# Attention, top-k and a small MLP on one core: another order of the score products, an earlier start of the next keys, and other forms of VectorE's side steps

## The chip, the cores and the metric

The kernel runs on one NeuronCore of a Trainium2 chip. The metric is device time in microseconds (us) of one launch, the median of several runs. The profile is one further execution, taken by the hardware profiler. The engines are called PE (TensorE; PEld is its weight load), DVE (VectorE), ACT (ScalarE), POOL (GpSimd) and SP (SyncE, which here only issues DMAs).

## The reference

Four batches are computed, each with 12288 queries of 128 channels. The keys and values are 4x4 means of a 384x32 grid, multiplied by one 128x128 matrix, so there are 768 of them per batch, and keys equal values.

```python
kv_flat = kv.reshape(B, H // 4, 4, W // 4, 4, C).mean(axis=(2, 4)).reshape(B, -1, C) @ w_sr
s = (q @ kv_flat.transpose(0, 2, 1)) / np.sqrt(C)
a = np.exp(s - s.max(-1, keepdims=True)); a /= a.sum(-1, keepdims=True) + 1e-09
x = a @ kv_flat                                   # (4, 12288, 128)
scores = np.einsum('bsd,d->bs', x, w_gate)        # then, per batch, the 128 highest rows:
xe = x[b, top_idx]; ye = np.maximum(xe @ w1, 0.0) @ w2
out[b, top_idx] = xe + ye / (1.0 + np.exp(-scores[b, top_idx]))[:, None]
```

## The kernel before

The queries are taken in blocks of 256 (two tiles of 128), 48 blocks to a batch, 192 in all. The main loop (from line 732) does one block `i` per turn, and every engine executes its instructions in exactly the order of this program text: the class `InOrder` chains them, and its one call site is line 56, which is why every row of the profile says L56. "Block 2.4" below is block 4 of batch 2, both counted from 0.

In turn `i` the engines do the following. DVE takes the row maximum of block i's scores (`s_max`, tile `m`). PE multiplies attention and values of block i-4 (`AV`, tiles `at` and `vx`, into the two PSUM banks `o_two`), first the high halves (12 products of 259 columns), then the low halves (12 of 130 columns). PE then computes the scores of block i+1 (`S`, into three PSUM banks, `s`), in four parts: part 3 of 512 columns, part 2 of 256, then, after two transposes, part 1 of 256 and part 0 of 512. Each part is the sum of three products, because a score is wanted to nearly fp32 exactness: one fp32r product of the rounded operands (`kh` and `qh`, called HIGH in the change) and two bf16 products of the remainders (`kl` with `qb`, which is the upper half of `qh` read as bf16, and `kb` with `ql`; called LOW). The two transposes (`turn_pe`, rows `s<-cst,am`) turn a 256-column share of block i's exponentials in batches 0 to 2; in batch 3 there are none (`TURN`, line 41) and DMA turns everything. ACT takes the exponentials (`exp`, tile `am`) and their fp16 high halves, POOL subtracts these for the low halves (`hl`, its longest step) and splits queries (`ql`, in even blocks), SP issues the DMA transposes (`turn`), the loads and the stores.

```python
for i, (w, x) in enumerate(high + low if part in (2, 0) else low + high):
    r = pe.matmul(s_flat[n % 2][:, lo:hi], w[:, q], x[:, k], start=(i == 0), stop=(i == 2))
```

Three side jobs are generators. Each stops at named points ("pe", "ev", "up", "g", "t", "cmp", "v", "d"), and `at_point` in the main loop lets the front one of each list go one step on where its point's name comes up, so that a job is spread over many blocks. The "d" point stands at the end of a turn, behind POOL's `hl`.

- `next_keys` (lists `prep` and `vals`) makes the next batch's keys and values: POOL adds up the loaded grid (`kv_sum`), six steps to each of six key tiles, one step a block; PE projects (`key_tile`); at the end `v_split` finds a power-of-two scale per batch and splits the values into fp16 high and low halves (`vx`), with one ACT and two POOL instructions in each of four steps. For batches 2 and 3 the adds wait for six "d" points first (line 350). `AV` of the first block of a batch, four blocks into the batch, needs all of `vx`.
- `topk` (list `select`) is started at the end of block 3 of the following batch. It sets `th` and `tl` on POOL, makes integer keys of the scores on DVE at the "d" point of block 4 (`key`, two instructions), and then searches the threshold, one bit in two or so blocks' points, until about block 37.
- `pick` continues it: it finds the positions of the 128 rows with small products and compares (`ge`, `oh`, `rj`, `idx`), gathers the rows by an indirect DMA of POOL, and runs the MLP. Its last sum is `y * g` on ACT (`xo`), `+ xe` on POOL one step later, and the indirect store of POOL one step after that. For batches 0 and 1 this end falls into blocks 2 to 4 of the batch after the next; for batch 2 it falls into the kernel's tail (`choose` with `drain`).

Batch 3's own selection (`choose`) is the tail, after the last block.

Of the kernel before, what the change touches and what calls it, by code (L numbers as in the profile page):

```python
# [6 lines left out]
F32 = mybir.dt.float32  # L7
# [3 lines left out]
I32 = mybir.dt.int32  # L11
U32 = mybir.dt.uint32
U16 = mybir.dt.uint16
AF = mybir.ActivationFunctionType
ALU = mybir.AluOpType
# [4 lines left out]
P = 128  # L20
# [6 lines left out]
JPC = CHUNK // P  # L27
# [7 lines left out]
NCOL = N // P  # L35
# [7 lines left out]
class InOrder:  # L43


    last = {}
# [24 lines left out]
def attention_topk_mlp(ctx, tc, a, outs, capacity):  # L71
# [108 lines left out]
    def v_split(b):  # L180
# [11 lines left out]
        dve.tensor_scalar(out=mg, in0=mg, scalar1=2.0 ** -96, scalar2=None, op0=ALU.max)  # L192
        dve.tensor_scalar(out=sg[:, 0:2].bitcast(I32), in0=mg.bitcast(I32), scalar1=0x7F800000, scalar2=0x7F800000, op0=ALU.bitwise_and, op1=ALU.bitwise_xor)
        yield "d"
        dve.tensor_scalar(out=sg[:, 0:2], in0=sg[:, 0:2], scalar1=4096.0, scalar2=None, op0=ALU.mult)
# [19 lines left out]
    def first_keys():  # L215
# [85 lines left out]
        S(1)  # L301
# [35 lines left out]
    def next_keys(b):  # L337
# [12 lines left out]
        lead, wait = (2, 0) if b == 1 else (1, 6)  # L350
# [57 lines left out]
    st = {}  # L408
# [15 lines left out]
    def S(n, parts=(0, 1, 2, 3), apart=()):  # L424
        b, blk = blocks[n]
        kh, kl, kb = (kvset[b][x] for x in ("kh", "kl", "kb"))
        qh, qb, ql = qsplit[b, blk]
        assert b == 0 or kvset[b].get("split") == KT
        for part in parts:
            lo, hi, j, k0 = ((0, 512, 0, 0), (512, 768, 0, 512), (768, 1024, 1, 0), (1024, 1536, 1, 256))[part]  # L430
            q = slice(j * P, (j + 1) * P)
            k = slice(k0, k0 + hi - lo)
            low, high = [(qb, kl), (ql, kb)], [(qh, kh)]
            for i, (w, x) in enumerate(high + low if part in (2, 0) else low + high):
                r = pe.matmul(s_flat[n % 2][:, lo:hi], w[:, q], x[:, k], start=(i == 0), stop=(i == 2))
                for y in apart:
                    tc.declare_no_dep(r.ins, y, reason="other banks")

    def s_max(n):
        m = sm.tile([P, QT], F32, name="m")  # L440
        dve.tensor_reduce(out=m, in_=s_flat[n % 2].rearrange("p (j k) -> p j k", j=QT), axis=AX.X, op=ALU.max, negate=True)
        st[n] = {"m": m}
# [145 lines left out]
    def pick(b, mask):  # L588
# [25 lines left out]
        for j0 in range(0, capacity, P):  # L614
# [5 lines left out]
            if j0:  # L620
                yield "d"
                jr = tk.tile([P, P], DT, name="jr")
                dve.tensor_scalar(out=jr, in0=small, scalar1=float(j0), scalar2=None, op0=ALU.add)
            for s in range(2):
                dve.tensor_scalar(out=ge[0:NCOL, s], in0=jr[0:NCOL], scalar1=ecol[0:NCOL, s:s + 1], scalar2=None, op0=ALU.is_ge)
# [20 lines left out]
            dve.scalar_tensor_tensor(out=rj, in0=jcol, scalar=float(j0), in1=row[:, 0:1], op0=ALU.add, op1=ALU.subtract)  # L646
# [5 lines left out]
            dve.scalar_tensor_tensor(out=idx, in0=pj, scalar=float(JPC), in1=row[:, 1:2], op0=ALU.mult, op1=ALU.add)  # L652
# [46 lines left out]
            if last:  # L699
                dve.scalar_tensor_tensor(out=xo[0:n], in0=y_ps[0:n], scalar=g[0:n], in1=xe[0:n], op0=ALU.mult, op1=ALU.add)  # L700
            else:
                act.activation(xo[0:n], y_ps[0:n], AF.Copy, scale=g[0:n])
                yield "d"
                pool.tensor_tensor(out=xo[0:n], in0=xo[0:n], in1=xe[0:n], op=ALU.add)
# [27 lines left out]
    for i in range(nb):  # L732
# [32 lines left out]
        if more:  # L765
            if not old:
                warm(12, s_flat[(i + 1) % 2][:, 1024:1024 + P], bank0 + bank1)
            S(i + 1, (3,), bank0 + bank1)
            S(i + 1, (2,), bank0)
# [4 lines left out]
        if more:  # L774
            S(i + 1, (1,), bank0)
            S(i + 1, (0,))
# [289 lines left out]
```

## Time and profile before

| | us |
|---|---|
| median of 3 runs | 937.86 (934.89 to 938.34) |
| the profiled execution | 938.39 |
| its span, first to last instruction | 936.5 |
| PE busy in the span | 878.3 (94%) |
| DVE busy | 805.6 (86%) |
| POOL busy | 749.0 (80%) |
| ACT busy | 740.7 (79%) |
| mean granted TensorE clock | 0.991 of 2.4 GHz |

A busy PE counts each product until its modelled end, and successive products overlap; how fast PE really goes is read from the distance between starts. Idle time of an engine costs nothing unless another one waits for it.

### The profile page before, as it was taken

The numbers are of one execution on the slowest core, as the hardware profiler recorded it, in microseconds if no ns is written. First come the engines' busy times: TensorE is split into PE (matmuls) and PEld (weight loads), VectorE is DVE, ScalarE is ACT, GpSimd is POOL, SyncE is SP. The second block draws the span as 40 slices with busy tenths as digits, with TensorE's granted clock in tenths as the row PEclk, the third lists the DMA queues.
The fourth block names the chain that finished last, engine by engine and source line by source line (L and its number), as shares of the span: only waits on it lengthen the run. The fifth ranks groups of instructions, "written<-read, shape, count | busy, mean of one in ns | idle before, by whom it ended". The sixth has DMA issues, their size and how long they took to land.

```text
span 936.5 us, 21381 instructions
## 1 busy us (share of the span) xinstructions
PE 878.3 (94%) x7785; PEld 685.6 (73%) x7785; DVE 805.6 (86%) x1929; ACT 740.7 (79%) x1139; POOL 749.0 (80%) x489
## 2 busy tenths in 40 slices
PE   4899999999999999999989999999997999999966
PEld 3577777777777777777767777777785777777766
DVE  5788888898898998999878999999978999999943
ACT  2788888889888887888868888888896999888821
POOL 2699999979788988987886998989887777777732
PEclk9999999999999999999999999999999999999989
DMA  8999999999999999999998999999998999999970
GB/s 318 292 204 232 254 232 243 226 206 202 219 213 224 243 225 230 253 213 253 215 213 181 248 215 230 242 239 241 228 201 189 243 219 250 243 250 259 237 163 27
DMA packets 564125, 211.12 MB, mean 225 GB/s; under 512 B 532368, under 2 KB 533648, under 8 KB 563376
## 3 DMA queue, kind: packets, MB, share of 16 engines
q1 hardware_dynamic: 563696, 209.06, 107.7%
q8 instruction: 62, 1.02, 0.5%
q0 software_dynamic: 320, 0.66, 0.3%
q14 instruction: 47, 0.39, 0.1%
HBM read 52.04 MB, written 25.49 MB: 83 GB/s over the span
## 4 chain that ended last, share of the span: by engine, by line
PE 59%; DVE 20%; DMA 8%; ACT 5%; POOL 4%; issue 2%; DVEq 0%; POOLq 0%; SPq 0%; another core or an unknown queue 0%; ACTq 0%
PE s L56 32%; PE o_two L56 27%; DVE m L56 8%; DMA at<-hl 7%; ACT am L56 3%; POOL hl L56 3%; DVE o_two L56 2%; DVE rz L56 2%; DVE hl L56 1%; DVE x L56 1%; ACT hl L56 1%; DVE key L56 1%; DMA kv_raw<-in_kv 1%; DVE at L56 1%; POOL ql L56 1%
## 5 line engine op out<-in xcount | busy, mean ns | idle before, releaser
L56 POOL TENSOR_TENSOR hl<-am,hl 128x1280 bf16<-128x1280 f32 x192 | 504.3, 2627 | 133.0 <-ACT hl L56 102.4
L56 PE MATMUL o_two<-vx,at 128*128 128x259 f16 (+1 forms) x4548 | 424.1, 247 | 17.0 <-DMA at<-hl 8.6
L56 PEld LDWEIGHTS <-at 128*128 128x128 f16 (+1 forms) x4656 | 365.3, 98 | 101.9 <-DMA at<-hl 18.5
L56 ACT ACTIVATE am<-s,m 128x512 f32<-128x512 f32 (+1 forms) x528 | 358.3, 706 | 62.3 <-DVE m L56 46.3
L56 DVE TENSOR_REDUCE m<-s 128x2 f32<-128x1536 f32 x192 | 336.2, 1751 | 12.5 <-PE s L56 11.5
L56 PE MATMUL s<-kl,qh 128*128 128x512 bf16 (+1 forms) x769 | 253.0, 332 | 0.0
L56 PE MATMUL s<-kh,qh 128*128 128x512 f32 (+1 forms) x769 | 251.5, 408 | 1.4 <-ACT kh L56 0.7
L56 PE MATMUL s<-kb,ql 128*128 128x512 bf16 (+1 forms) x769 | 248.7, 327 | 1.3 <-POOL ql L56 1.3
L56 ACT CAST hl<-am 128x1280 f16<-128x1280 f32 x192 | 241.6, 1258 | 6.1
L56 PEld LDWEIGHTS s<-kh,qh 128*128 128x128 f32 x769 | 131.6, 191 | 31.8 <-ACT kh L56 1.0
L56 DVE TENSOR_REDUCE o_two<-o_two 128x258 f32<-128x516 f32 x188 | 128.3, 683 | 0.0
L56 POOL TENSOR_TENSOR ql<-q_raw,qh 128x512 bf16<-128x512 f32 x96 | 122.7, 1278 | 3.4 <-ACT qh L56 3.4
L56 PEld LDWEIGHTS <-qh 128*128 128x128 bf16 x769 | 74.9, 97 | 62.1 <-issue 61.4
L56 ACT CAST at<-s 128x256 f16<-128x256 f32 x144 | 53.7, 373 | 64.4 <-PE s L56 64.4
L56 DVE TENSOR_SCALAR rz<-o_two,sg 128x2 f32<-128x2 f32 x189 | 41.1, 217 | 47.2 <-PE o_two L56 45.8
L56 PEld LDWEIGHTS <-ql 128*128 128x128 bf16 x769 | 76.2, 99 | 5.2 <-POOL ql L56 2.1
L56 DVE TENSOR_TENSOR x<-o_two,rz 128x256 f32<-128x256 f32 x189 | 78.3, 414 | 0.0
L56 DVE TENSOR_TENSOR at<-s,at 128x256 bf16<-128x256 f32 x144 | 60.7, 422 | 10.4 <-ACT at L56 4.9
L56 PE MATMUL s<-cst,am 128*128 128x128 f32 x288 | 56.2, 277 | 10.0 <-ACT am L56 9.7
L56 ACT CAST qh<-q_raw 128x512 fp32r<-128x512 f32 x96 | 58.8, 613 | 0.0
L56 POOL TENSOR_TENSOR kv_sum<-kv_raw 128x256 f32<-128x256 f32 x72 | 52.6, 730 | 0.0
L56 PEld LDWEIGHTS s<-cst,am 128*128 128x128 f32 x288 | 34.8, 141 | 17.0 <-ACT am L56 15.5
(163 smaller groups left out, 545.8 us busy)
## 6 DMA issues: line engine op xcount, KB each, us to landing
out<-x SPq DMA_DIRECT2D x96, 256.0 KB, 3.1
q_raw<-in_q SPq DMA_DIRECT2D x94, 256.0 KB, 3.7
kv_raw<-in_kv SPq DMA_DIRECT2D x37, 512.0 KB, 4.7
at<-hl SPq DMA_TRANSPOSE x384, 4.0
kv_raw<-in_kv SPq DMA_DIRECT2D x5, 1024.0 KB, 9.5
w<-in_w SPq DMA_DIRECT2D x2, 512.0 KB, 12.1
kv_raw<-in_kv SPq DMA_DIRECT2D x2, 256.0 KB, 5.4
q_raw<-in_q SPq DMA_DIRECT2D x1, 512.0 KB, 5.5
```

What stands on the lines that cost most here:

```text
L56: r = f(*args, **kwargs)
```

## The change

The score products of a turn are put in another order: LOW of parts 3 and 2, HIGH of parts 3 and 2, the two transposes, HIGH of parts 1 and 0, LOW of parts 1 and 0; `S` now makes one part's HIGH or LOW products at a call. `next_keys` of batches 2 and 3 waits for five "d" points instead of six. In `v_split` three DVE instructions on two columns become two each on one column. In `pick`, `ge` also writes a row sum that nobody reads (`took`), `rj` and `idx` become `tensor_scalar` with a per-partition scalar instead of `scalar_tensor_tensor` with a second tensor, and the last sum of the MLP becomes one DVE instruction that reads the product from PSUM, for all batches; with it one "d" step goes.

```diff
--- before.py
+++ after.py
@@ -189,10 +189,14 @@
         mg = kvs.tile([P, 2], F32, name="mg")
         dve.tensor_reduce(out=mg, in_=ps, axis=AX.X, op=ALU.max)
         yield "d"
-        dve.tensor_scalar(out=mg, in0=mg, scalar1=2.0 ** -96, scalar2=None, op0=ALU.max)
-        dve.tensor_scalar(out=sg[:, 0:2].bitcast(I32), in0=mg.bitcast(I32), scalar1=0x7F800000, scalar2=0x7F800000, op0=ALU.bitwise_and, op1=ALU.bitwise_xor)
+        one = [slice(i, i + 1) for i in range(2)]
+        for i in one:
+            dve.tensor_scalar(out=mg[:, i], in0=mg[:, i], scalar1=2.0 ** -96, scalar2=None, op0=ALU.max)
+        for i in one:
+            dve.tensor_scalar(out=sg[:, i].bitcast(I32), in0=mg[:, i].bitcast(I32), scalar1=0x7F800000, scalar2=0x7F800000, op0=ALU.bitwise_and, op1=ALU.bitwise_xor)
         yield "d"
-        dve.tensor_scalar(out=sg[:, 0:2], in0=sg[:, 0:2], scalar1=4096.0, scalar2=None, op0=ALU.mult)
+        for i in one:
+            dve.tensor_scalar(out=sg[:, i], in0=sg[:, i], scalar1=4096.0, scalar2=None, op0=ALU.mult)
         dve.tensor_scalar(out=sg[:, 3:4], in0=sg[:, 0:1], scalar1=float(TAPS), scalar2=None, op0=ALU.mult)
         yield "d"
         parts = [(raw[:, :, 2 * P:2 * P + 1], slice(0, KT), slice(C, VL), 1)]
@@ -298,7 +302,10 @@
         first([(512, 768, 0, 512, True), (1280, 1536, 1, 512, True)])
         project_v(4)
         project_v(5)
-        S(1)
+        for parts in (0, 1), (2, 3):
+            for term in LOW, HIGH:
+                for part in parts:
+                    S(1, part, term)
 
     v_ps = o_two[:, :, 0:3 * (C + 1)].rearrange("p b (t c) -> p b t c", t=3)
 
@@ -347,7 +354,7 @@
                 pend.extend([lambda: None,
                              lambda: (split_k(b, 2 * pair, 2 * pair + 2, 0), split_k(b, 2 * pair, 2 * pair + 2, 1))])
 
-        lead, wait = (2, 0) if b == 1 else (1, 6)
+        lead, wait = (2, 0) if b == 1 else (1, 5)
         raws[0] = load_kv(b, 0, 1 if b == 1 else -2)
         if b == 1:
             raws[1] = load_kv(b, 1)
@@ -421,25 +428,28 @@
 
     blocks = [(b, blk) for b in range(B) for blk in range(NBLK)]
 
-    def S(n, parts=(0, 1, 2, 3), apart=()):
+    LOW, HIGH = 0, 1
+
+    def S(n, part, terms, apart=()):
         b, blk = blocks[n]
         kh, kl, kb = (kvset[b][x] for x in ("kh", "kl", "kb"))
         qh, qb, ql = qsplit[b, blk]
         assert b == 0 or kvset[b].get("split") == KT
-        for part in parts:
-            lo, hi, j, k0 = ((0, 512, 0, 0), (512, 768, 0, 512), (768, 1024, 1, 0), (1024, 1536, 1, 256))[part]
-            q = slice(j * P, (j + 1) * P)
-            k = slice(k0, k0 + hi - lo)
-            low, high = [(qb, kl), (ql, kb)], [(qh, kh)]
-            for i, (w, x) in enumerate(high + low if part in (2, 0) else low + high):
-                r = pe.matmul(s_flat[n % 2][:, lo:hi], w[:, q], x[:, k], start=(i == 0), stop=(i == 2))
-                for y in apart:
-                    tc.declare_no_dep(r.ins, y, reason="other banks")
+        lo, hi, j, k0 = ((0, 512, 0, 0), (512, 768, 0, 512), (768, 1024, 1, 0), (1024, 1536, 1, 256))[part]
+        q = slice(j * P, (j + 1) * P)
+        k = slice(k0, k0 + hi - lo)
+        begun = ("S", part) in st.setdefault(n, {})
+        st[n]["S", part] = True
+        mm = [(qh, kh)] if terms == HIGH else [(qb, kl), (ql, kb)]
+        for i, (w, x) in enumerate(mm):
+            r = pe.matmul(s_flat[n % 2][:, lo:hi], w[:, q], x[:, k], start=not begun and i == 0, stop=begun and i == len(mm) - 1)
+            for y in apart:
+                tc.declare_no_dep(r.ins, y, reason="other banks")
 
     def s_max(n):
         m = sm.tile([P, QT], F32, name="m")
         dve.tensor_reduce(out=m, in_=s_flat[n % 2].rearrange("p (j k) -> p j k", j=QT), axis=AX.X, op=ALU.max, negate=True)
-        st[n] = {"m": m}
+        st.setdefault(n, {})["m"] = m
 
     def by_pe(n):
         return TURN[blocks[n][0]][n % 2] > 0
@@ -621,8 +631,9 @@
                 yield "d"
                 jr = tk.tile([P, P], DT, name="jr")
                 dve.tensor_scalar(out=jr, in0=small, scalar1=float(j0), scalar2=None, op0=ALU.add)
+            took = tk.tile([P, 2], F32, name="took")
             for s in range(2):
-                dve.tensor_scalar(out=ge[0:NCOL, s], in0=jr[0:NCOL], scalar1=ecol[0:NCOL, s:s + 1], scalar2=None, op0=ALU.is_ge)
+                dve.tensor_scalar(out=ge[0:NCOL, s], in0=jr[0:NCOL], scalar1=ecol[0:NCOL, s:s + 1], scalar2=None, op0=ALU.is_ge, op1=ALU.add, accum_out=took[0:NCOL, s:s + 1])
             yield "d"
             for s in range(2):
                 dve.scalar_tensor_tensor(out=oh[0:NCOL, s], in0=jr[0:NCOL], scalar=ecx[0:NCOL, s:s + 1], in1=ge[0:NCOL, s], op0=ALU.is_ge, op1=ALU.subtract)
@@ -643,13 +654,16 @@
                 sel, row = sel[:, 0:P], sel[:, P:P + 2]
             yield "d"
             rj = tk.tile([P, 1], F32, name="rj")
-            dve.scalar_tensor_tensor(out=rj, in0=jcol, scalar=float(j0), in1=row[:, 0:1], op0=ALU.add, op1=ALU.subtract)
+            if j0:
+                dve.scalar_tensor_tensor(out=rj, in0=jcol, scalar=float(j0), in1=row[:, 0:1], op0=ALU.add, op1=ALU.subtract)
+            else:
+                dve.tensor_scalar(out=rj, in0=row[:, 0:1], scalar1=-1.0, scalar2=jcol, op0=ALU.mult, op1=ALU.add)
             yield "cmp"
             pj = tk.tile([P, 1], F32, name="pj")
             dve.tensor_scalar(out=pick_out, in0=sel, scalar1=rj, scalar2=None, op0=ALU.is_le, op1=ALU.add, accum_out=pj)
             yield "d"
             idx = tk.tile([P, 1], U32, name="idx")
-            dve.scalar_tensor_tensor(out=idx, in0=pj, scalar=float(JPC), in1=row[:, 1:2], op0=ALU.mult, op1=ALU.add)
+            dve.tensor_scalar(out=idx, in0=pj, scalar1=float(JPC), scalar2=row[:, 1:2], op0=ALU.mult, op1=ALU.add)
             xe = tk.tile([P, C], F32, name="xe")
             pool.indirect_dma_start(out=xe[0:n], out_offset=None, in_=outs[b],
                                          in_offset=bass.IndirectOffsetOnAxis(ap=idx[0:n], axis=0))
@@ -696,12 +710,7 @@
             dve.reciprocal(g[0:n], g[0:n])
             yield "ev"
             xo = tk.tile([P, C], F32, name="xo")
-            if last:
-                dve.scalar_tensor_tensor(out=xo[0:n], in0=y_ps[0:n], scalar=g[0:n], in1=xe[0:n], op0=ALU.mult, op1=ALU.add)
-            else:
-                act.activation(xo[0:n], y_ps[0:n], AF.Copy, scale=g[0:n])
-                yield "d"
-                pool.tensor_tensor(out=xo[0:n], in0=xo[0:n], in1=xe[0:n], op=ALU.add)
+            dve.scalar_tensor_tensor(out=xo[0:n], in0=y_ps[0:n], scalar=g[0:n], in1=xe[0:n], op0=ALU.mult, op1=ALU.add)
             yield "d"
             pool.indirect_dma_start(out=outs[b], out_offset=bass.IndirectOffsetOnAxis(ap=idx[0:n], axis=0),
                                          in_=xo[0:n], in_offset=None)
@@ -765,15 +774,16 @@
         if more:
             if not old:
                 warm(12, s_flat[(i + 1) % 2][:, 1024:1024 + P], bank0 + bank1)
-            S(i + 1, (3,), bank0 + bank1)
-            S(i + 1, (2,), bank0)
+            free = {3: bank0 + bank1, 2: bank0, 1: bank0, 0: ()}
+            for part, term in ((3, LOW), (2, LOW), (3, HIGH), (2, HIGH)):
+                S(i + 1, part, term, free[part])
         exp(i, 2 if by_pe(i) else 1)
         if by_pe(i):
             turn_pe(i)
         exp(i, 1 if by_pe(i) else 2)
         if more:
-            S(i + 1, (1,), bank0)
-            S(i + 1, (0,))
+            for part, term in ((1, HIGH), (0, HIGH), (1, LOW), (0, LOW)):
+                S(i + 1, part, term, free[part])
         to_high(i, 1)
         if old:
             sums(i - LAG)
```

## Rows read from the trace of the kernel before

**Rows 1.** The page, busy time by engine, and DMA's busy tenths in 40 slices.
```profile
PE 878.3 (94%) x7785; PEld 685.6 (73%) x7785; DVE 805.6 (86%) x1929; ACT 740.7 (79%) x1139; POOL 749.0 (80%) x489
...
DMA  8999999999999999999998999999998999999970
```

**Rows 2.** Windows: from:to, us, busy us by engine, granted clock, DMA share, GB/s.
```profile
113.83:135.23 21.40, 21.40 (x192) 16.87 (x191) 18.29 (x36) 18.70 (x29) 19.65 (x14) 1.00 1.17 231
747.54:776.14 28.60, 28.60 (x261) 22.21 (x259) 27.87 (x78) 26.26 (x39) 23.29 (x12) 1.00 1.19 229
254.26:268.20 13.94, 13.10 (x117) 10.08 (x116) 12.85 (x29) 11.31 (x18) 9.30 (x7) 1.00 1.28 224
479.56:499.39 19.83, 14.91 (x118) 10.85 (x117) 15.86 (x30) 11.43 (x18) 13.33 (x11) 0.91 0.81 178
703.67:722.79 19.12, 14.15 (x111) 10.60 (x110) 16.05 (x30) 12.56 (x19) 13.01 (x11) 0.91 0.77 180
```

**Rows 3.** Timeline of PE in block 2.4 and ahead of 2.5.
```profile
481.14 1.74 PE L56 MATMUL o_two<-vx,at 128*128 128x259 f16 x20 [1.17 <-POOL vx L56]
...
491.93 0.53 PE L56 MATMUL s<-cst,am 128*128 128x128 f32 x2 [3.75 <-ACT am L56]
```

**Rows 4.** Timeline of DVE in block 2.4.
```profile
484.90 1.84 DVE L56 TENSOR_SCALAR key<-sc 128x96 int32<-128x96 int32 x1
486.78 2.65 DVE L56 TENSOR_TENSOR key<-key,sc 128x96 int32<-128x96 int32 x1
```

**Rows 5.** Timeline of POOL in block 2.4.
```profile
485.38 1.29 POOL L56 TENSOR_TENSOR ql<-q_raw,qh 128x512 bf16<-128x512 f32 x1
486.70 2.62 POOL L56 TENSOR_TENSOR hl<-am,hl 128x1280 bf16<-128x1280 f32 x1
```

**Rows 6.** Timeline of DVE in block 1.4.
```profile
258.26 0.33 DVE L56 TENSOR_SCALAR key<-sc 128x96 int32<-128x96 int32 x1
258.63 1.25 DVE L56 TENSOR_TENSOR key<-key,sc 128x96 int32<-128x96 int32 x1
```

**Rows 7.** Timeline of PE in block 0.10: start, us, instruction, count.
```profile
67.70 0.38 PE L56 MATMUL s<-kl,qh 128*128 128x512 bf16 x1
67.91 0.38 PE L56 MATMUL s<-kb,ql 128*128 128x512 bf16 x1
...
68.60 0.27 PE L56 MATMUL s<-kb,ql 128*128 128x256 bf16 x1
68.71 0.38 PE L56 MATMUL s<-cst,am 128*128 128x128 f32 x2
...
69.04 0.27 PE L56 MATMUL s<-kb,ql 128*128 128x256 bf16 x1
...
69.95 0.72 PE L56 MATMUL o_two<-vx,at 128*128 128x259 f16 x5
```

**Rows 8.** The page, weight loads: busy, mean ns, idle before, and what ended it.
```profile
L56 PEld LDWEIGHTS <-qh 128*128 128x128 bf16 x769 | 74.9, 97 | 62.1 <-issue 61.4
```

**Rows 9.** Timeline of DVE in the tail.
```profile
921.20 0.29 DVE L56 COPY kv_raw<-s 128x128 f32<-128x128 f32 x1 [2.54 <-PE s L56]
```

**Rows 10.** By tile: count, least/median/most ns, first and last start.
```profile
L56 DVE TENSOR_SCALAR ge<-jrow,ecol x6: 242/458/1310, 429.9 to 869.9; 96x128 bf16<-96x128 bf16 x6
...
L56 DVE SCALAR_TENSOR_TENSOR idx<-pj,sel x3: 353/1006/1008, 445.2 to 883.3; 128x1 uint32<-128x1 f32 x3
...
L56 DVE TENSOR_SCALAR_CACHE_REDUCE junk<-key,th x48: 302/312/315, 262.9 to 779.7; 128x96 bf16<-128x96 uint16 x48
...
L56 DVE TENSOR_SCALAR th<-up,th x48: 202/203/206, 267.4 to 783.5; 128x1 f32<-128x1 f32 x48
```

**Rows 11.** Timeline of PE, first and last of five transposes kept waiting.
```profile
209.07 0.44 PE L56 MATMUL s<-cst,am 128*128 128x128 f32 x2 [0.54 <-ACT am L56]
...
673.75 0.44 PE L56 MATMUL s<-cst,am 128*128 128x128 f32 x2 [0.40 <-ACT am L56]
```

**Rows 12.** Waits, all of the span: us in total, times, longest us.
```profile
PE o_two L56 <- DMA at<-hl: 8.6, 13, 1.3
```

## The prediction

> **What bounds the kernel now.** I read the page first: PE is busy for 94% of the span, DVE for 86%, POOL for 80%, and the DMA line stands at 9 nearly throughout [rows 1]. A mean over stages does not say who is late in each, so I went to stretches next. In batch 0, blocks 20 to 24 take 21.40 us, 4.28 a block, with PE busy for all of it and DVE for 18.29: PE sets the pace [rows 2]. In batch 3, seven blocks take 28.60 us, 4.09 each; PE is busy for all of it too, but DVE for 27.87, so only 0.10 a block lies between the two [rows 2]. Then I looked for blocks that take longer. The largest losses are at the turns of the batches: blocks 4 to 6 take 13.94 us in batch 1, but 19.83 in batch 2 and 19.12 in batch 3, the granted clock falls to 0.91 of 2.4 GHz there, and PE is busy for only 14.91 and 14.15 us [rows 2]. The timeline of PE in block 2.4 names what it waits for: 1.17 us for POOL's `vx`, and then 3.75 us, ahead of the transposes, for ACT's exponentials [rows 3]. They need block 2.5's `m`, which stands behind DVE's two `key` steps, and these took 1.84 and 2.65 us [rows 4], the second up to the end of POOL's `hl` (486.70 + 2.62) [rows 5]. The same second step took 1.25 us in block 1.4 [rows 6].
>
> **The score order.** In block 0.10 I compare starts with columns, one a cycle at 2.4 GHz (granted 1.00 there [rows 2]): 512 columns are 0.213 us, and the first product takes 0.21, from 67.70 to 67.91 [rows 7]. From `kb` at 67.91 to the second LOW product behind the fp32r pair at 68.60 are 1536 columns, 0.64, and it takes 0.69. From `kb` at 69.04 to AV at 69.95 are 2048 columns, 0.853, and it takes 0.91 [rows 7]. So the two changes into fp32r and the two out of it cost 0.05 + 0.06; I take 0.09 for a block, as a few ns are lost behind any product. One cause can be seen: the bf16 loads of `qh` stood idle for 61.4 us in all [rows 8]; only half of the 769 follow an fp32r product, so that is 0.16 before each, the load beginning when the fp32r product ends. The new order has one fp32r stretch in place of two: half of 0.09 goes, 0.045 a block, 6.5 us over the 144 blocks of batches 0 to 2.
>
> New are two seams, fp32r to transpose and transpose to fp32r. No row shows either. From below I put them at nothing, a loader that runs ahead as it does between two bf16 products. From above, a load that stands wholly uncovered: two transposes and a LOW product follow each other 0.11 apart, from 68.71 to 69.04 [rows 7], so a load of these kinds cannot last longer than that; 0.22 for both. I take 0.01 for the pair, since the second of two fp32r products is loaded without a visible gap inside the 0.69 and a transpose has fp32 weights as it has: 1.4 us. Batch 3 has no transposes, and its saving is capped by DVE at 0.10 a block; I take 1.0 us for its 48. The score order thus gives 6.5 - 1.4 + 1.0 = 6.1 us; its bounds are 17 (144 + 48 times 0.09) and a loss of 25 (144 times 0.22 - 0.045).
>
> The Trainium skill ("TensorE: Matmul & The Clock Gate", Part 2, "What happens when you issue a matmul") says that PE's queue pulls a weight load ahead of running matmuls when it goes to the background buffer. By that rule no load would wait for a product, and gathering the fp32r products would spare none; the 0.16 us of [rows 8] contradict it for bf16 behind fp32r. By the rule the sum would be 926 (first rival).
>
> **Earlier keys and the MLP's sum.** With five waits everything in `next_keys` of batches 2 and 3 comes a block earlier, its kv loads on SP's queue too; they stay in the same order against the transposes, but change places between a query load and a store. AV had waited 1.17 us for `vx` when it began at 481.14 [rows 3]; a block earlier (4.28 us [rows 2]) it is ready, so that goes, and I take the same for batch 3. From POOL's queue ahead of the `key` steps go the two steps of `vx`, the add of `xo`, and, as the store is now a "d" point earlier, the indirect DMA. Then blocks 2.4 and 3.4 meet what 1.4 met: there the first `key` step slips in between two POOL steps and only the second waits [rows 6]. Against 13.94 us in batch 1, batch 2 loses 5.9; batch 3, whose three undisturbed blocks take 12.3 and which would keep the 1.1 that batch 1 loses (13.94 less three times 4.28), loses 5.8 [rows 2]. Together 11.7; I take 11. Bounds: 2.3 (the two waits for `vx` alone) and 13.9 (the `key` steps free as well).
>
> ACT loses its `xo` step. DVE gets one that reads PSUM; the nearest row, a 128-column copy from PSUM, is 0.29 [rows 9], I take 0.35. It stands behind `m` and waits for the MLP's last products; behind it are `up`, `g` and the sums, which in those blocks wait for PE's AV anyway. In the tail it comes ahead of five small steps, and DVE sat idle for 2.54 us there before the copy at 921.20 [rows 9]; between nothing and 0.4 us late, I take 0.1.
>
> **VectorE's side steps.** `ge` took 0.24 to 1.31 us and `idx` 0.35 to 1.01 [rows 10]: at the long end they wait out a POOL step, and the next `m`, the exponentials and the transposes come later by that. Five times PE then idles ahead of its transposes, the first time 0.54 us, behind a scale step of `v_split`, the last time 0.40, behind `idx` [rows 11]; 0.57 in the mean, 2.9 in all. The forms that come in their place never wait: `th`, a `tensor_scalar` with a scalar per partition, took 0.20 to 0.21 in all of 48, the compare with a sum 0.30 to 0.32 [rows 10]. I take all of the 2.9. Bounds: nothing, if the next POOL step catches another DVE step instead, and 5.7, twice as much, if the blocks behind gain too. The nine instructions added by splitting are hidden, since DVE has (21.40 - 18.29) / 5 = 0.6 us a block to spare in batch 0 [rows 2]; uncovered they would be 0.2 each at the price of `th`, 1.8 us.
>
> **Given back.** SP and the DMAs are near their own limit: PE waited for `at` 13 times for 8.6 us [rows 12], though never in block after block. A faster PE meets them more often: I take 1.5 us, bounds 0 and 5.
>
> **Sum.** The profiled execution took 938.39 us, its span 936.5; the median of the runs is 937.86, so nothing separates the two. 938.4 - 6.1 - 11 - 2.9 + 0.1 + 1.5 = **920 us**.
>
> **Rivals.** (1) The seams around the transposes cost what the piece spares: four changes of kind a block, as now, only at other places. For it speaks that transposes stand in the middle of the piece; against it, that their loads follow bf16 without a gap [rows 7]. PE's 6.1 goes: 926. (2) The stall at the turns stays: DVE's first `key` step is again passed over by two POOL steps in a row, for `ql` and `hl` still follow each other in that block. In block 2.4 POOL's `vx` and indirect DMA were not what the second step waited for, it was `hl` [rows 4, 5]. Then only the two waits for `vx` go: 938.4 - 6.1 - 2.3 - 2.9 + 1.6 = 929. (3) Slower: an fp32r product blocks every load behind it, and the loads of the transposes and of the fp32r products behind them stand uncovered, 0.22 a block in 144 blocks; 938.4 + 25.2 - 1.0 - 11 - 2.9 + 1.6 = 950. It decides from 0.14 us for both seams on, where 144 times (0.14 - 0.045) eats the other 13.3. For it speaks the 0.16 of [rows 8]; against it the second fp32r product, whose load does run ahead.
>
> **Chances.** The forecast 0.63, with 912 to 927 as its own range; rival 1 0.15, rival 2 0.14, rival 3 0.08. About 0.5% (4.7 us) is what a measurement of this kernel can tell from no change. Faster by more than that, under 933.2: all of the forecast and of rivals 1 and 2 but for where both hold or DMA waits add to them, 0.83. Within 0.5%: 0.10. Slower: 0.07, most of rival 3. The range that leaves two in ten out reaches from 910 to 934.
>
> **What would show it.** Right: in PE's timeline of a steady block the order kl, kb, kl, kb, kh, kh, transposes, kh, kh and then LOW, with about 4.23 us between the starts of `m`; blocks 4 to 6 near 14 us in batch 2 and near 13.5 in batch 3, PE without a wait for `vx`; no `ge` or `idx` over 0.4 us. Wrong: a gap ahead of the transposes' loads, a steady block of 4.28 or more, a `key` step of 2 us or more in block 2.4 or 3.4, or waits for `at` well over 10 us.

## The result: 1.1% faster, and the profile after

The changed kernel takes 928.72 us in the median of 20 runs (921.36 to 932.35), the kernel before 939.03 in as many (931.31 to 943.12): ratio 0.9889, 95% interval 0.987 to 0.9908. Measured twice more beside other kernels, it stood at 0.9909 (0.9876 to 0.9942) and 0.9884 (0.985 to 0.9918). The forecast was 920: right in sign, and within the wide range of 910 to 934, but outside the forecast's own range of 912 to 927. 18 us less were forecast and 10 came.

The page after, first row of part 1 and the loads of `qh` (busy, mean ns, idle before, and what ended it):

```profile
PE 867.4 (93%) x7665; PEld 684.0 (74%) x7785; DVE 795.8 (86%) x1947; ACT 739.0 (80%) x1136; POOL 747.3 (81%) x486
...
L56 PEld LDWEIGHTS <-qh 128*128 128x128 bf16 x769 | 74.8, 97 | 52.8 <-issue 29.4
```

The idle time of these loads that nothing but the engine's own queue explains fell from 61.4 us [rows 8] to 29.4. But that figure adds up only the long gaps, those over 0.15 us. All the idle time before the loads of `qh` fell from 62.1 to 52.8, and that before the loads of `ql` rose, before and then after:

```profile
L56 PEld LDWEIGHTS <-ql 128*128 128x128 bf16 x769 | 76.2, 99 | 5.2 <-POOL ql L56 2.1 <-POOL kl L56 0.3 <-issue 0.3
...
L56 PEld LDWEIGHTS <-ql 128*128 128x128 bf16 x769 | 75.4, 98 | 33.5 <-POOL ql L56 7.6 <-issue 0.8
```

So the idle time mostly changed its place: span less busy time of PEld is 250.9 us before and 244.1 after. We shall see that PE got some 3 us.

Windows of the kernel after, for blocks 0.20 to 0.24, seven blocks of batch 3, and blocks 4 to 6 of batches 1, 2 and 3 (columns as in [rows 2]):

```profile
112.83:134.88 22.05, 21.34 (x189) 16.82 (x191) 18.30 (x36) 18.69 (x29) 19.68 (x14) 1.00 1.17 222
737.53:766.00 28.47, 28.31 (x259) 22.28 (x260) 27.74 (x78) 26.29 (x39) 23.31 (x12) 1.00 1.22 234
252.56:266.50 13.94, 12.97 (x115) 10.12 (x116) 12.86 (x29) 11.33 (x18) 9.28 (x7) 1.00 1.16 215
476.98:490.86 13.88, 12.95 (x116) 10.10 (x117) 12.81 (x30) 11.33 (x18) 10.36 (x8) 1.00 1.08 198
699.83:713.23 13.40, 12.53 (x112) 9.77 (x113) 12.84 (x29) 11.32 (x18) 9.78 (x7) 1.00 1.11 224
```

Against [rows 2] the turns of batches 2 and 3 fall from 19.83 and 19.12 us to 13.88 and 13.40, and the granted clock is 1.00 there. Batch 3's seven blocks fall only from 28.60 to 28.47. The first window holds one wait for a DMA, so it can't be compared as a whole; its other four blocks take 4.265 each in place of 4.28. Between the starts of blocks 0.26 and 0.31, which hold no such wait, are 21.39 us before and 21.31 after.

Cut at the starts of `m`, the two profiled executions differ so:

| stretch | before | after | difference |
|---|---|---|---|
| start to 0.5 | 48.32 | 47.52 | -0.80 |
| 0.5 to 0.38 | 143.89 | 144.14 | +0.25 |
| 0.38 to 1.4 (`v_split`) | 62.05 | 60.90 | -1.15 |
| 1.4 to 1.7 | 13.94 | 13.94 | 0 |
| 1.7 to 1.39 | 148.79 | 149.42 | +0.63 |
| 1.39 to 2.4 (`pick`, `v_split`, MLP) | 62.57 | 61.06 | -1.51 |
| 2.4 to 2.7 | 19.83 | 13.88 | -5.95 |
| 2.7 to 2.39 | 143.11 | 148.77 | **+5.66** |
| 2.39 to 3.4 (`pick`, `v_split`, MLP) | 61.17 | 60.20 | -0.97 |
| 3.4 to 3.7 | 19.12 | 13.40 | -5.72 |
| 3.7 to 3.38 | 129.08 | 128.88 | -0.20 |
| 3.38 to the end | 84.63 | 85.99 | +1.36 |

The start is scatter (over the kernels below block 0.5 begins at 46.0 to 48.4 us), and so is the end (82.2 to 86.2 us over these kernels): in the tail the granted clock was 0.86 in the mean against 0.89. The surprise is the row in bold: batch 2 gained 6 us at its turn and lost as much in the next 32 blocks. PE's waits in that stretch, before and then after (engine and line: us in total, times, longest us):

```profile
PE s L56 <- ACT am L56: 0.7, 1, 0.7
PE o_two L56 <- DMA at<-hl: 0.4, 2, 0.2
PE o_two L56 <- DVE at L56: 0.2, 1, 0.2
```

```profile
PE o_two L56 <- DMA at<-hl: 3.1, 4, 1.3
PE s L56 <- POOL ql L56: 1.6, 4, 0.4
PE s L56 <- ACT am L56: 1.0, 3, 0.6
```

`ql` is new in this list. POOL's timeline of the kernel after from the end of block 2.10 on (start, us, instruction) tells why:

```profile
507.85 1.28 POOL L56 TENSOR_TENSOR kv_sum<-kv_sum 128x512 f32<-128x512 f32 x1
509.07 1.28 POOL L56 TENSOR_TENSOR ql<-q_raw,qh 128x512 bf16<-128x512 f32 x1
510.30 2.65 POOL L56 TENSOR_TENSOR hl<-am,hl 128x1280 bf16<-128x1280 f32 x1
512.88 0.64 POOL L56 TENSOR_TENSOR kv_sum<-kv_sum 128x256 f32<-128x256 f32 x1
513.60 0.42 POOL L56 TENSOR_TENSOR pooled<-kv_sum 128x128 f32<-128x128 f32 x1
514.18 2.62 POOL L56 TENSOR_TENSOR hl<-am,hl 128x1280 bf16<-128x1280 f32 x1 [0.16 <-ACT hl L56]
```

and PE's in the same place:

```profile
510.41 0.39 PE L56 MATMUL s<-kb,ql 128*128 128x512 bf16 x1 [0.38 <-POOL ql L56]
```

`next_keys` gives POOL six steps to a key tile, one a block, and the fifth is an add of 512 columns. `ql` comes in every second block. An add moved by one block changes sides: here the add (1.28), `ql` (1.28) and `hl` (2.65) follow each other, 5.2 us of steps where a block has 4.3, and `ql` ends at 510.35, after PE wants it. In the kernel before the same add stood in a block without `ql`; its POOL timeline in block 2.12:

```profile
518.31 2.64 POOL L56 TENSOR_TENSOR hl<-am,hl 128x1280 bf16<-128x1280 f32 x1
520.89 1.29 POOL L56 TENSOR_TENSOR kv_sum<-kv_sum 128x512 f32<-128x512 f32 x1
522.35 2.62 POOL L56 TENSOR_TENSOR hl<-am,hl 128x1280 bf16<-128x1280 f32 x1 [0.17 <-ACT hl L56]
```

The wait for `ql` is only half of it. After, blocks 2.11 and 2.12 take 4.63 and 5.15 us; the blocks of the same steps before, 2.12 and 2.13, take 4.30 and 4.74. Of the 0.74 lost, 0.33 lie in the block with the wait and 0.41 in the next: there POOL ends the key tile's last step, `pooled`, 0.46 later in the block, since it stands behind the late `hl`, and PE projects the tile 0.30 later. The weight loads of these products, in all key tiles, before and then after:

```profile
L56 PEld LDWEIGHTS s<-pooled,w_k 128*128 128x128 f32 x36 | 5.4, 189 | 0.3
...
L56 PEld LDWEIGHTS s<-pooled,w_k 128*128 128x128 f32 x36 | 5.4, 188 | 4.3 <-POOL pooled L56 4.2
```

The turn itself went as forecast. DVE's two `key` steps in block 2.4, to be compared with [rows 4]:

```profile
480.98 0.29 DVE L56 TENSOR_SCALAR key<-sc 128x96 int32<-128x96 int32 x1
481.30 1.24 DVE L56 TENSOR_TENSOR key<-key,sc 128x96 int32<-128x96 int32 x1
```

The side steps too (by tile: count, least/median/most ns; compare [rows 10]):

```profile
L56 DVE TENSOR_SCALAR_CACHE_REDUCE ge<-jrow,ecol x6: 331/334/336, 428.7 to 860.2; 96x128 bf16<-96x128 bf16 x6
...
L56 DVE SCALAR_TENSOR_TENSOR oh<-jrow,ecx,ge x6: 335/454/1424, 433.9 to 865.6; 96x128 bf16<-96x128 bf16 x6
```

```profile
L56 DVE TENSOR_SCALAR idx<-pj,sel x3: 203/204/205, 443.5 to 873.8; 128x1 uint32<-128x1 f32 x3
```

`oh`, which the change left alone, still takes up to 1.42 us.

### The profile page after: what moved, and what is told of

Same layout as the page of the kernel before. It is cut to its first block, busy times and chain, and to the rows that moved or that the text cites. A ratio compares the mean times of both kernels' runs of the same rounds, so it can differ in the third digit from the quotient of the medians.

```text
span 928.1 us, 21277 instructions
## 1 busy us (share of the span) xinstructions
PE 867.4 (93%) x7665; PEld 684.0 (74%) x7785; DVE 795.8 (86%) x1947; ACT 739.0 (80%) x1136; POOL 747.3 (81%) x486
## 4 chain that ended last, share of the span: by engine, by line
PE 57%; POOL 11%; DVE 10%; DMA 9%; issue 7%; ACT 5%; SPq 0%; POOLq 0%; DVEq 0%; another core or an unknown queue 0%; ACTq 0%
PE s L56 30%; PE o_two L56 26%; DMA at<-hl 7%; POOL hl L56 5%; DVE m L56 4%; POOL kv_sum L56 3%; ACT am L56 3%; POOL ql L56 2%; DMA kv_raw<-in_kv 2%; ACT hl L56 1%; DVE o_two L56 1%; DVE hl L56 1%; DVE rz L56 1%; DVE x L56 1%; DVE kv_raw L56 1%
## 5 line engine op out<-in xcount | busy, mean ns | idle before, releaser
L56 PE MATMUL s<-kb,ql 128*128 128x256 bf16 (+1 forms) x741 | 230.4, 324 | 8.6 <-POOL ql L56 3.9
L56 PE MATMUL s<-kh,qh 128*128 128x512 f32 (+1 forms) x769 | 215.7, 376 | 1.2 <-ACT kh L56 0.7
L56 PE MATMUL s<-kl,qh 128*128 128x512 bf16 (+1 forms) x677 | 209.0, 321 | 1.7 <-POOL ql L56 0.4
L56 PEld LDWEIGHTS s<-kh,qh 128*128 128x128 f32 x769 | 116.5, 191 | 6.2 <-ACT kh L56 0.9
L56 PEld LDWEIGHTS <-qh 128*128 128x128 bf16 x769 | 74.8, 97 | 52.8 <-issue 29.4
L56 PEld LDWEIGHTS s<-cst,am 128*128 128x128 f32 x288 | 35.7, 140 | 17.5 <-ACT am L56 11.7
```

The source lines that it names most:

```text
L56: r = f(*args, **kwargs)
```

## The experiments

All were run in five rounds beside the kernel before, four to a chip; ratios are to it. A count that recurs below is the length of a stretch less PE's waits for the DMA transposes (`at`) in it, because these waits move from run to run: their sum over the whole execution was 8.6 us in the profile of before and 9.7, 15.1 and 15.2 in three of the kernel after.

**Six waits again.**

```diff
-        lead, wait = (2, 0) if b == 1 else (1, 5)
+        lead, wait = (2, 0) if b == 1 else (1, 6)
```

> The kernel after with six waits again, the rest as it is. Theory: the stall at the turns of batches 2 and 3 (11.7 us) went because of the fifth wait alone, and that wait cost some 8 us by putting POOL's 512-column add of the grid into the blocks in which it also splits queries. Then the stall is back (blocks 2.4 to 2.6 and 3.4 to 3.6 near 19.5 us) but PE waits for ql for under 1.5 us in all, so about 3 us above the kernel after: ratio to before 0.993. Rival: the sum of the MLP on DVE alone freed the key steps. Then blocks 2.4 to 2.6 stay near 15 us with a wait for vx of 1.2, and the time is 5 to 6 us below the kernel after: ratio 0.983.

Measured: 932.32 us, ratio 0.9911 (0.9881 to 0.9942). Blocks 4 to 6 of batches 2 and 3 (windows), and the first `key` step of block 3.4 in the kernel before:

```profile
476.27:491.64 15.37, 13.22 (x118) 10.11 (x117) 12.96 (x29) 11.32 (x18) 11.82 (x10) 1.00 1.04 214
694.31:713.08 18.77, 14.30 (x113) 10.82 (x112) 15.62 (x30) 12.80 (x19) 12.63 (x10) 0.91 0.77 182
...
708.80 4.60 DVE L56 TENSOR_SCALAR key<-sc 128x96 int32<-128x96 int32 x1
```

The rival is right in batch 2, where 15.37 remain of 19.83, and not in batch 3, where 18.77 of 19.12 remain and the first `key` step takes 4.18 us, nearly the 4.60 of before. The 32 blocks behind the turn of batch 2 take 142.0 us less `at`, not 145.7: the loss there does go with the sixth wait.

**Four waits.** The same line with `(1, 4)`, run on two chips.

> The kernel after with four waits. Theory: an even shift keeps POOL's 512-column add out of the query blocks, so PE waits for ql for under 1.5 us in all instead of 4.3, blocks 7 to 39 of batch 2 take 4 us less than in the kernel after, and the same in batch 1, while the turns stay near 14 us: 6 to 8 us below the kernel after, ratio to before 0.981. Rival: what blocks 7 to 39 lost comes from the score order and from late DMA transposes, whatever POOL adds when; then no difference to the kernel after: 0.989. A third way: two blocks earlier brings the loads of the grid into the last loads of the batch before, and PE waits for at for 12 us or more: above 0.989.

> Four waits again, beside the kernel after on one chip. Theory: 6 to 8 us below the kernel after, 0.981 to 0.983 of before; blocks 7 to 39 of batch 2 at 142.4, of batch 1 at 142.5 to 144.5, less waits for at. Rival: the first result came from another chip, no difference.

Measured: 924.79 us, ratio **0.981** (0.9785 to 0.9835), and 926.23, **0.9819** (0.9778 to 0.986), where the kernel after had 931.39 beside it. The turns stay at 13.87 and 13.40. POOL's timeline has the long add between two `hl` again, and PE's waits in blocks 7 to 39 of batch 2 (second chip) hold no `ql`:

```profile
505.98 1.29 POOL L56 TENSOR_TENSOR kv_sum<-kv_sum 128x512 f32<-128x512 f32 x1
507.43 2.63 POOL L56 TENSOR_TENSOR hl<-am,hl 128x1280 bf16<-128x1280 f32 x1 [0.15 <-ACT hl L56]
```

```profile
PE o_two L56 <- DMA at<-hl: 3.4, 5, 1.0
PE s L56 <- ACT am L56: 1.2, 1, 1.2
```

Over the kernels, the 32 blocks 7 to 38 less waits for `at`, in us, and of them the ten in which five key tiles are finished (the block in which PE projects a key tile, and the one ahead of it):

| waits | kernel | batch 1 | batch 2 | ten of batch 1 | ten of batch 2 |
|---|---|---|---|---|---|
| 6 | before | 142.6 | 142.7 | 46.3 | 46.3 |
| 6 | six waits again | 142.8 | 142.0 | 46.2 | 46.0 |
| 6 | before, the score order alone (below) | 144.5 | 142.3 | 46.2 | 46.0 |
| 4 | four waits, two chips | 144.4, 143.2 | 142.4, 142.6 | 45.6, 45.6 | 45.6, 45.6 |
| 5 | after, three profiles | 145.8, 146.2, 148.1 | 145.7, 145.3, 145.6 | 49.1, 49.3, 49.2 | 48.5, 48.6, 48.8 |
| 5 | five waits, the long add in halves (below) | 146.2 | 143.0 | 46.3 | 46.2 |

Only the odd count with the whole add is dear. In the ten blocks, which hardly scatter, it costs 3 us in batch 1 and 2.5 in batch 2 against six waits, and 3.6 and 3.0 against four: about 6 together. The other blocks of batch 1 differ by up to 3.6 us between kernels without regard to the count. Four waits is the best version that was run. It beats the kernel before on both chips; against the kernel after, its interval on the first chip lies below all three of that kernel's, and on the second, beside it, the two intervals overlap by 0.001.

**The long add in two halves, with five waits.**

```diff
-            adds += [[(u[:, :, 0:4], u[:, :, 0:4], u[:, :, 4:8])], [(u[:, :, 0:2], u[:, :, 0:2], u[:, :, 2:4]),
+            fold = [(u[:, k:k + 64, 0:4], u[:, k:k + 64, 0:4], u[:, k:k + 64, 4:8]) for k in (0, 64)]
+            adds[3] += fold[:1]
+            adds += [fold[1:], [(u[:, :, 0:2], u[:, :, 0:2], u[:, :, 2:4]),
```

> The kernel after, five waits, with the 512-column add of each key tile cut into two of 256: the first half goes into the block before, which has no query split, the second stays. Theory: the loss of blocks 7 to 39 is POOL's block with the 512-column add and the query split together (5.2 us of POOL work in a block of 4.26); with 4.6 instead, PE's waits for ql fall from 4.1 to under 2.5 us and these blocks to 143 to 144 us each, less waits for at; 4 to 6 us below the kernel after. Rival: the odd count of waits hurts through other meetings (the key tile's products and ACT's copies in another block); then they stay at 145 to 146 and the time at that of the kernel after.

Measured: 934.42 us, ratio 0.9916 (0.9884 to 0.9948), 3 us above the kernel after (the intervals overlap) where 4 to 6 below were expected. As a whole, batch 2 did as the theory says, 143.0 less `at` in place of 145.6, and batch 1 stayed at 146.2. But the ten blocks of the table fall to the level of six waits in both batches, 46.3 and 46.2, and no wait for `ql` is left in either: with the count still odd, it is the long add that decides. Batch 1's other blocks took 3 us more than in the first profile of the kernel after, 1.8 of them one wait for DVE's `m`. Batch 0, whose adds begin without any wait and were on the good side, now has `ql` waits of its own (1.7 us in five), and the waits for `at` came to 19.4. The edit moved the meeting to another batch, and so gained nothing.

**The MLP's sum on ACT and POOL again.**

```diff
-            dve.scalar_tensor_tensor(out=xo[0:n], in0=y_ps[0:n], scalar=g[0:n], in1=xe[0:n], op0=ALU.mult, op1=ALU.add)
+            if last:
+                dve.scalar_tensor_tensor(out=xo[0:n], in0=y_ps[0:n], scalar=g[0:n], in1=xe[0:n], op0=ALU.mult, op1=ALU.add)
+            else:
+                act.activation(xo[0:n], y_ps[0:n], AF.Copy, scale=g[0:n])
+                yield "d"
+                pool.tensor_tensor(out=xo[0:n], in0=xo[0:n], in1=xe[0:n], op=ALU.add)
```

> The kernel after with the MLP's last sum on ACT and POOL again, and its one more d point. Theory: the earlier keys alone take vx out of the way, but the add of xo and the indirect store stand ahead of the key steps again in blocks 2.4 and 3.4; if these decide, the second key step takes over 2 us and both turns lose 4 us each: 8 us slower than the kernel after, ratio to before 0.997. Rival: the turn depends on the two steps of vx only; blocks 2.4 to 2.6 stay near 14 us and the time is that of the kernel after, 0.989.

Measured: 931.14 us, ratio 0.9894 (0.987 to 0.9917), that of the kernel after. The turns are even a little shorter (windows):

```profile
476.74:490.14 13.40, 13.02 (x117) 10.12 (x116) 11.83 (x29) 11.31 (x18) 10.75 (x9) 1.00 1.06 203
699.72:712.97 13.25, 12.57 (x114) 9.67 (x113) 11.88 (x29) 11.91 (x19) 11.20 (x9) 1.00 1.06 204
```

The indirect store now stands behind `hl`, and the `key` steps of block 2.4, which come as `hl` ends, take 0.21 and 0.26 us. So the rival holds: with five waits the turn is free, and the MLP's sum on DVE adds nothing to it.

**The side steps of before** in the kernel after, and the kernel after beside them.

```diff
...
-                dve.tensor_scalar(out=ge[0:NCOL, s], in0=jr[0:NCOL], scalar1=ecol[0:NCOL, s:s + 1], scalar2=None, op0=ALU.is_ge, op1=ALU.add, accum_out=took[0:NCOL, s:s + 1])
+                dve.tensor_scalar(out=ge[0:NCOL, s], in0=jr[0:NCOL], scalar1=ecol[0:NCOL, s:s + 1], scalar2=None, op0=ALU.is_ge)
...
-            dve.tensor_scalar(out=idx, in0=pj, scalar1=float(JPC), scalar2=row[:, 1:2], op0=ALU.mult, op1=ALU.add)
+            dve.scalar_tensor_tensor(out=idx, in0=pj, scalar=float(JPC), in1=row[:, 1:2], op0=ALU.mult, op1=ALU.add)
...
```

> The kernel after with the side steps of before (v_split on two columns, ge without a sum, rj and idx with two tensors). Forecast's term: 2.9 us slower than the kernel after, ratio 0.992, with ge up to 1.3 and idx up to 1.0 us again and PE ahead of its transposes waiting 0.4 to 0.8 us five times more. Rival: those waits are taken up by the blocks behind, because POOL or DMA were late anyway; ratio 0.989, no difference.

> The kernel after itself, on the chip of the other three, as their measure. Both theories: ratio 0.989, since nothing is changed; its sum of waits for at tells how far that wait moves by itself (9.7 us in its first profile, 8.6 in that of before): if it comes out between 8 and 14, the 1.5 us given back are inside that movement.

Measured: 936.73 us, 0.9946 (0.9919 to 0.9973), against 932.51, 0.9909 (0.9876 to 0.9942): 4 us by the medians, with intervals that overlap. The traces are clearer: the stretches 0.38 to 1.4, 1.39 to 2.4 and 2.39 to 3.4 take 61.95, 62.26 and 61.36 us against 60.90, 61.09 and 60.22, which is 3.36 in all. Nearly all of it is `v_split`'s: the first of these stretches holds `v_split` without `pick` and loses 1.05, the other two 1.17 and 1.14. Its scale steps on two columns, in this run:

```profile
L56 DVE TENSOR_SCALAR sg<-sg x6: 153/156/1103, 205.7 to 680.9; 128x2 f32<-128x2 f32 x3, 128x1 f32<-128x1 f32 x3
...
L56 DVE TENSOR_SCALAR sg<-mg x3: 169/1198/1202, 201.9 to 675.7; 128x2 int32<-128x2 int32 x3
```

The three long ones end within 0.03 us of the end of POOL's `ql`; on one column none took over 0.16 in the kernel after. `ge` took 0.24 to 0.65 us in this run and `idx` 0.15 to 0.35, less than before [rows 10]; what their new forms are worth where they would wait longer, no run shows by itself.

**The score order alone, and undone.** The kernel before with the new `S` and its order; the kernel after with the order of before (the edit shown).

```diff
-            for part, term in ((3, LOW), (2, LOW), (3, HIGH), (2, HIGH)):
+            for part, term in ((3, LOW), (3, HIGH), (2, HIGH), (2, LOW)):
...
-            for part, term in ((1, HIGH), (0, HIGH), (1, LOW), (0, LOW)):
+            for part, term in ((1, LOW), (1, HIGH), (0, HIGH), (0, LOW)):
```

> The kernel before with the new score order alone. Forecast's term: 6.1 us less, ratio 0.9935, steady blocks of 4.24 in batch 0 and 4.07 in batch 3. Theory from the trace after: 4.263 and 4.066, so 144 times 0.015 and 48 times 0.02, 3 us less, ratio 0.9967. Both leave blocks 2.4 to 2.6 and 3.4 to 3.6 at 19 to 20 us.

> The kernel after with the score order of before (part by part) in the main loop, the rest as it is. The forecast's term: 6.1 us slower than the kernel after, ratio to before 0.9955, steady block of batch 0 4.31 against 4.265. Theory from the trace after: the new order spares only 0.015 us a block in batches 0 to 2 and 0.02 in batch 3, so 3 us slower, ratio 0.992, steady block 4.28 and 4.09.

Measured: alone 942.9 us against 941.33, ratio 1.0005 (0.9968 to 1.0041); undone 930.84, 0.9895 (0.9869 to 0.9921), where the kernel after has 0.9884 to 0.9909. The steady blocks are 4.26 and 4.065 with the new order, 4.27 to 4.28 and 4.09 with the old, as the trace after had it: 0.015 and 0.02 a block, 3 us. Of these the whole time shows nothing that can be told from no change; alone, PE's waits for `at` came to 12.0 us against 8.6, which would hide them. The forecast's 6.1 is excluded by both intervals.

**One fp32r stretch a block.** Both with four waits: the transposes behind all four HIGH products, or ahead of them (`KL` and `KB` are the two LOW products taken singly). Of the edits the order is shown.

```diff
...
-            for part, term in ((3, LOW), (2, LOW), (3, HIGH), (2, HIGH)):
+            for part, term in ((3, LOW), (2, LOW), (3, HIGH), (2, HIGH), (1, HIGH), (0, HIGH)):
...
-            for part, term in ((1, HIGH), (0, HIGH), (1, LOW), (0, LOW)):
+            for part, term in ((1, LOW), (0, LOW)):
```

> Four waits, and the two transposes behind all four HIGH products, so that batches 0 to 2 have one fp32r stretch a block as batch 3 has. Theory 1 (the forecast's half: each stretch has its own price, which the two seams at the transposes took back): a steady block of batch 0 drops from 4.263 to 4.24 or less, 3 us or more in 144 blocks, ratio 0.978 against the 0.981 of four waits. Theory 2 (most of the price is paid behind each fp32r product, about 0.01 each, wherever it stands): a steady block of 4.25 to 4.26, at most 2 us, ratio 0.979 to 0.981. A third way: the transposes come 0.33 us later and ACT's copy of them and its last exponential with them; then m waits and the block is longer than 4.263.

```diff
...
-            for part, term in ((3, LOW), (2, LOW), (3, HIGH), (2, HIGH)):
+            for part, term in ((3, LOW), (2, LOW), (0, KL)):
...
-            for part, term in ((1, HIGH), (0, HIGH), (1, LOW), (0, LOW)):
+            for part, term in ((3, HIGH), (2, HIGH), (0, HIGH), (1, HIGH), (1, LOW), (0, KB)):
```

> Four waits and one fp32r stretch a block, with the transposes ahead of it: LOW of parts 3 and 2, kl of part 0, transposes, all four HIGH, LOW of part 1, kb of part 0. Theory 1 (a stretch has a price of its own): 4.23 in all steady blocks of batch 0, as every second one of the kernel with the transposes behind, and nothing later on ACT; 4 us below four waits, ratio 0.977. Theory 2 (the price is paid behind each fp32r product): 4.255, 0 to 1 us below. A third way: bank 0 is wanted 0.5 us earlier, and PE waits for DVE's copies of the key tiles and of the search out of it: above four waits.

> The kernel after once more, as the measure of the three beside it: 0.989 to 0.991 of before. Blocks 7 to 39 of batches 1 and 2, less PE's waits for at in them, take 145 to 146 us each, where the kernel before took 142.6 and 142.7.

Measured: 929.42 us, 0.9861 (0.9822 to 0.9901), and 930.43, 0.9862 (0.9823 to 0.9901); the kernel after beside the second 931.39, 0.9884. Neither beats four waits alone. PE's timelines of a steady block of batch 0 price the changes of kind. Kernel after:

```profile
150.48 0.27 PE L56 MATMUL s<-kb,ql 128*128 128x256 bf16 x1
150.51 0.60 PE L56 MATMUL s<-kh,qh 128*128 128x512 f32 x2
150.95 0.38 PE L56 MATMUL s<-cst,am 128*128 128x128 f32 x2
151.09 0.59 PE L56 MATMUL s<-kh,qh 128*128 128x256 f32 x2
151.52 0.28 PE L56 MATMUL s<-kl,qh 128*128 128x256 bf16 x1
...
152.18 0.50 PE L56 MATMUL o_two<-vx,at 128*128 128x259 f16 x3
```

Transposes behind:

```profile
151.02 0.27 PE L56 MATMUL s<-kb,ql 128*128 128x256 bf16 x1
151.05 0.94 PE L56 MATMUL s<-kh,qh 128*128 128x512 f32 x4
151.82 0.38 PE L56 MATMUL s<-cst,am 128*128 128x128 f32 x2
152.04 0.27 PE L56 MATMUL s<-kl,qh 128*128 128x256 bf16 x1
...
152.69 0.27 PE L56 MATMUL o_two<-vx,at 128*128 128x259 f16 x1
```

Transposes ahead:

```profile
149.71 0.38 PE L56 MATMUL s<-cst,am 128*128 128x128 f32 x2
149.85 0.95 PE L56 MATMUL s<-kh,qh 128*128 128x512 f32 x4
150.65 0.28 PE L56 MATMUL s<-kl,qh 128*128 128x256 bf16 x1
...
151.09 0.27 PE L56 MATMUL o_two<-vx,at 128*128 128x259 f16 x1
```

Over the columns at one a cycle of 2.4 GHz, and 0.22 for the two transposes, the time from the product ahead of the first fp32r one to AV is longer by 0.05 + 0.06 = 0.11 us before [rows 7]; by 0.04 + 0.03 + 0.02 = 0.09 after; by 0.05 + 0.01 = 0.06 with the transposes behind; by 0.08 + 0.01 = 0.09 with them ahead, where it is counted from the transposes. What orders these is how often bf16 follows fp32r directly: twice, once, never, once, at about 0.02 each (the rows resolve 0.01; the steady blocks give 0.016 for the one that the change removes). The rest, 0.05 to 0.06, stays where the four fp32r products are gathered and no bf16 product follows them. It isn't the step into them either: by the starts of the single products with the transposes behind (means of batch 0), the four are 0.023, 0.010, 0.010 and 0.018 us longer than their 512, 256, 256 and 512 columns, where a bf16 product among its like is 0.0025 longer. So it is theirs, about a tenth of their columns' time. The long gaps before the loads of `qh` go with the exits: 61.4, 29.4 and 7.0 us for two, one and none, the 7.0 being batch 3's, which has no transposes and so keeps one:

```profile
L56 PEld LDWEIGHTS <-qh 128*128 128x128 bf16 x769 | 74.9, 97 | 28.5 <-issue 7.0
```

The transposes behind do give the 4.23 us that theory 1 forecasts (blocks 0.26, 0.28 and 0.30), but in the blocks between, 4.48 and 4.49, the third way: ACT's copy of the transposes comes later, `hl` and then POOL's `ql` behind it, and PE's product with `ql` starts 0.45 us after its neighbour, not 0.22. In the form with the transposes ahead a steady block takes 4.27, so having one stretch was not what mattered. That form was 4 us above four waits beside it, by medians with intervals that overlap; why, if it is so, stays open.

## Why the prediction was right, and where it was off

The sign came from a right mechanism, the freed turns. That the time stayed within the outer range is owed to its width: the two large misses below, 6 and 3 us, point the same way.

**What bounds the kernel:** right. The turns were the largest losses, and removing them gave the largest gain.

**Earlier keys:** the term of 11 us measured 11.7 (5.95 + 5.72), the `key` steps of 0.29 and 1.24 us behave as in block 1.4, and the clock no longer falls. Rival 2 is refuted in the kernel after. The cause is narrower than I wrote: with the fifth wait the turns stayed free whichever other edit was undone, and the MLP's sum on DVE is worth nothing once the wait is there. Without it the other edits together freed most of batch 2's turn, and next to nothing of batch 3's.

**The step that failed by leaving something out** stands in the same part: "With five waits everything in `next_keys` of batches 2 and 3 comes a block earlier". I followed its loads on SP's queue and its last steps on POOL's, but not the thirty-six steps of adds in between, which pass from blocks with `ql` to blocks without it and back. That is +6 us in batches 1 and 2, shown by the counts of waits and by the add in halves. A row that warned of it was there: POOL had 19.65 of 21.40 us busy [rows 2], so a step of 1.28 (which no row ahead of the prediction shows) could hardly move to a block with another of 1.29 [rows 5] for nothing.

**The score order:** 6.1 us forecast, 3 by the steady blocks, and not to be told from nothing by the whole time. "Half of 0.09 goes" was the wrong step: I shared the loss out over changes of kind, two in and two out, but over half of it belongs to the fp32r products themselves. Beside that only bf16 behind fp32r costs, about 0.02 each, and the change removes one of two. The seams at the transposes, for which I took 0.01, are indeed cheap. So rival 1's price for this term was nearer and its reason wrong (that its total of 926 lies near the measured time is luck, as it lacks the adds' 6 us), and rival 3 didn't occur. "0.16 before each", the long gaps before the loads, led me to it: 32 us of these went, PE gained 3, and the loads as a whole stood idle for only 7 us less. What the Trainium skill says on loads that are pulled ahead ("TensorE: Matmul & The Clock Gate", Part 2, "What happens when you issue a matmul") would have made this term nothing. For bf16 behind fp32r the loads do stand idle [rows 8]; in the time of PE the 3 us of the steady blocks lie halfway between the rule's nothing and my 6.1, and the whole time, which shows none, is nearer to the rule.

**Side steps:** 2.9 forecast, 3.4 by the traces, but by another share than I wrote: about 1.05 of each stretch is `v_split`'s scale steps, which I named beside the first of the five waits alone, and `ge` and `idx` gave some 0.1 in two of them. **Tail:** the new sum took 0.35 us as estimated; what it does to the rest of the tail is within the tail's scatter.

**Given back:** 1.5 forecast. In the profiles shown the waits for `at` rose by 1.1, but by 6.5 in the two later ones of the kernel after. Since there is one profile of before, how much of this the change causes and how much is scatter stays open.

By these sizes the sum is 938.4 - 3 - 11.7 - 3.4 + 6 + 1 to 7, or 927 to 933; the profiled execution took 929.98. The forecast's own range, 912 to 927, missed it for the 6 us of the adds and the 3 of the score order.

## What to carry to other kernels

When a chain of steps, one a block, is moved by one block, lay every step of it against whatever else comes every second block on the same engine: an even move kept the pattern here and an odd one cost half of the gain. Price a change of order on TensorE by the distance between the starts of products, not by the idle time of one kind of weight loads: here its long gaps shrank by 32 us, the loads of another kind stood idle for 28 us more, and PE gained 3. And undo the parts one by one: two of the four edits here gave nearly the whole gain, and one of these two had a better setting a single number away.

## What the runs showed of the hardware

An fp32r product took more than one cycle a column where the granted clock was 1.00 of 2.4 GHz: four of 1536 columns gathered took 0.06 us over their 0.64, even where no bf16 product followed them. A bf16 product directly behind fp32r cost about 0.02 us more; between transposes and products of either kind no such price could be seen. DVE's scale steps took up to 1.20 us on two columns, and on one column never over 0.16.
